# Starting the frequency groups of batches 3 to 7 another 1.2 slots earlier

## The chip, the cores and the metric

One core of a Trainium2 chip runs the whole program. The metric is device time in microseconds (us) of one launch. Names of engines as in the profile: PE is the matmul engine, ACT, DVE and POOL are the scalar, vector and GpSimd engines, SP issues most DMAs.

## The reference

The input x is 8 batches of 3072 rows by 256 columns. Each batch is transformed along its rows to the frequency domain, multiplied there by a complex 256x256 matrix, given a bias, soft-thresholded and transformed back. The 24576 rows that come out pass through a feed-forward block with three maxed branches.

```
X = np.fft.rfft(x, axis=1);  Xr, Xi = X.real, X.imag
Yr = Xr @ w_r - Xi @ w_i + b_r
Yi = Xr @ w_i + Xi @ w_r + b_i
Y* = sign(Y*) * maximum(abs(Y*) - 0.01, 0)
y = np.fft.irfft(Yr + 1j * Yi, n=3072, axis=1)        # 24576 x 256 over all batches
h = maximum(maximum(y @ w1, y @ w2), y @ w3)          # 768 wide
out = h @ w_out
```

## The kernel before

**Tiling.** A batch's main loop has 48 slots (`SLOTS`): 8 chunks of 384 rows, and per chunk 6 blocks of 128 of the 768 hidden columns. In a slot PE does an up product into a tile `pu` (two halves of 6 matmuls, L184 to L186, with a relu by ACT at L1142 between them, which overwrites `pu`) and the down products (`pd`) of an earlier block. The maximum of three branches is taken by two relus and additions folded into the weights. `h` is taken out of `pu` by ACT (L1150) or, every third block, DVE (L1146), and split into two half-precision parts `hh`.

**The transform, between the slots.** A length of 3072 is done as 96 x 32. For batch b, in four steps:

- `stage_a` (L612): the 96-point part for one of 8 pieces of x: 12 matmuls of 48 rows (L625) into two tiles `pa`, emptied by two ACT copies `aq` (L632) and stored to DRAM. Before it DVE and ACT combine and split the piece (`xq` L575, `xhl`).
- `load_a`, `split_a` (`ab`, L694 and L697) and `stage_b` (L792): the 32-point part of a group of frequencies, 16 matmuls into one tile `px`. Four readers empty it: ACT `tt` and `s` (L805), DVE `tt` and `s` (L808). A batch has 12 groups k.
- `stage_w`, `stage_w2`: the weights, three small products into two tiles `py`, read by ACT `cs` (L883) and by DVE `u` (L893), which also adds the bias (L899) and applies the threshold (L837, L839); `finish_w` splits `u` into `vb`, first half on ACT, second on DVE.
- `stage_q` (L960): for every two groups, 12 matmuls into two tiles `pz`, emptied by two ACT copies `zs` (L966) and stored to DRAM. From there the main loop of the next 48 slots takes them in by chunk: `load_z`, `split_z` (`zh` on ACT, `zl` on DVE, then moves `ze<-zl` on SP), `inverse` (`pi` L1091, two tiles per chunk), then `y`, `yh`, `yl`.

**Buffers.** The 8 accumulation banks are three tags: `up` 3 (the tiles `pu`), `dn` 2 (`pd`), and `ff` 3. The tiles `px`, `py`, `pz`, `pa` and `pi` all go through `ff_tile` and so share the three `ff` buffers in the order in which they are issued: a tile gets the buffer of the third `ff` tile before it, when all readers of that one are through.

**What sets the order.** There is no dynamic choice. A table `events` holds (position in slots, function, argument), filled by `at`; `run_until(pos)` issues what is due at thirds of a slot. Second halves of splits wait in `later` for a third or two. Every engine then runs its own list in that order. Two rules of the table matter here (DFT batch b sits in the main loop's slots (b-1)*48 on; its x pieces one batch earlier):

- x pieces of batches 3 to 7, i = 0 to 7: base p = (b-2)*48 + 5.6*i; `stage_a` at p+1.
- groups k of batches 3 to 7: base p = (b-1)*48 - 1.2 + 2.72*(k+2); `stage_b` of group k+1 at p+1, `stage_w` of k at p+2, `stage_w2` at p+2.4, `finish_w` of k-1 at p+1.6, `split_a` of k+1 at p-2.2, `stage_q` of k-1 at p+4 (it acts for every second group), `load_a` of k+3 at p.

`load_z`, `split_z` and `inverse` are called in the main loop itself, at fixed blocks of a chunk, and are in no table.

Of the kernel before, what the change touches and what calls it, by code (L numbers as in the profile page):

```python
# [101 lines left out]
def fourier_maxout_kernel(  # L102
# [13 lines left out]
    SLOTS = NCH * NF  # L116
# [371 lines left out]
    def at(pos, fn, i, k=None, n=None):  # L488
        if n is None or 0 <= k < n:
            events.append((pos, len(events), fn, i))  # L490
# [487 lines left out]
    for q in range(EARLY, NB * NCH):  # L978
        b, i = divmod(q, NCH)
        p = i if b == 1 else 9 + 5.2 * i if b == 2 else (b - 2) * SLOTS + 5.6 * i  # L980
# [5 lines left out]
        if q >= HALF_X:  # L986
            p = 9 + 5 * i if b == 3 else (b - 3) * SLOTS + 5.5 * i + 5
# [3 lines left out]
                at(p + 1, scale_m, b)  # L991
    for b in range(1, NB):
        for k in range(-2, NJP + 1):
            p = 8 + 2.13 * (k + 2) if b == 1 else (b - 1) * SLOTS - (1.2 if b > 2 else 0.4) + 2.72 * (k + 2)
            for d, fn, i in (
                (0, load_a, k + 3), (-2.2 if b > 2 else -1.6, split_a, k + 1), (1.6, finish_w, k - 1),
                (1, stage_b, k + 1), (4 if k < NJP else 3, stage_q, k - 1), (2, stage_w, k), (2.4, stage_w2, k),
            ):
                at(p + d, fn, b * NJP + i, i, NJP)
            if k == -2:  # L1000
                at(p - (2.5 if b > 2 else 0), load_a, b * NJP)
# [530 lines left out]
```

## Time and profile before

| | |
|---|---|
| median of 3 runs | 1742.68 us (1740.84 to 1744.57) |
| profiled execution | 1737.65 us, its span 1735.9 us |
| PE busy | 1713.4 us, 99% of the span, granted clock 1.0 |
| DVE busy | 1269.0 us, 73% |
| ACT busy | 1169.1 us, 67% |
| POOL busy | 292.2 us, 17% |
| main loop's period | 207.18 us a batch (776.12 to 983.30 for the same `pa` block), 4.316 us a slot |

The main loops of batches 2, 3, 4 and 5 (545 to 752, 752 to 959, 959 to 1166 and 1166 to 1372 us) repeat one pattern: in each the groups of the next batch and the x pieces of the batch after that are run. The loop of batch 6 (1372 to 1569 us) has groups but no x pieces, the last one (1569 us on) neither. An engine that is busy 99% of the span shows what bounds the kernel; for the others the idle time before an instruction counts only where PE waits for what that instruction frees or makes.

### The profile page before, as it was taken

The page shows a single profiled execution, that of the slowest core. Times are in us where ns is not written, and L with a number is a line of the kernel's source. Part 1 is how long each engine was busy: PE and PEld are TensorE (multiplying, and loading weights), DVE is VectorE, ACT ScalarE, POOL GpSimd, SP SyncE. Part 2 cuts the span into 40 slices and gives each one's busy share as a digit, 9 for nine tenths or more (in the row PEclk, how much of TensorE's full clock was granted, in tenths as well). Part 3 has the DMA queues.
Part 4 walks back from the last instruction along what each step waited for, and adds up shares of the span by engine and source line. Part 5 has one row for each costly group of instructions (what it writes and reads, how often), then busy time and mean ns, then how long its engine had stood idle before and what let it go on. Part 6 is the DMA issues. An engine that isn't in the chain of part 4 may idle for free.

```text
span 1735.9 us, 42087 instructions
## 1 busy us (share of the span) xinstructions
PE 1713.4 (99%) x16171; PEld 1278.0 (74%) x16171; DVE 1269.0 (73%) x2690; ACT 1169.1 (67%) x2493; POOL 292.2 (17%) x523
## 2 busy tenths in 40 slices
PE   8999999999999999999999999999999999999998
PEld 5866777677776777777777777777777777778998
DVE  2887887687866788678876688757787467667775
ACT  4567676677766777667775777667776566666775
POOL 2101012111221212211221111211222110110000
PEclk9999999999999999999999999999999999999999
DMA  9866565577646767466766567555753443422121
GB/s 294 249 183 195 161 167 162 159 183 190 186 120 178 181 185 192 133 175 177 191 168 167 156 178 204 159 143 153 191 160 106 121 126 104 122 78 64 56 60 34
DMA packets 203863, 269.61 MB, mean 155 GB/s; under 512 B 31438, under 2 KB 153262, under 8 KB 203566
## 3 DMA queue, kind: packets, MB, share of 16 engines
q1 hardware_dynamic: 171294, 193.34, 42.4%
q0 software_dynamic: 24736, 66.62, 12.0%
q10 hardware_dynamic: 7632, 6.95, 1.4%
q8 instruction: 128, 2.10, 0.5%
q14 instruction: 73, 0.60, 0.1%
HBM read 124.31 MB, written 75.50 MB: 115 GB/s over the span
## 4 chain that ended last, share of the span: by engine, by line
PE 81%; DVE 9%; DMA 5%; ACT 4%; issue 1%; SPq 1%; ACTq 0%; POOL 0%; DVEq 0%; POOLq 0%
PE pu L184 11%; PE pu L186 11%; PE pu L185 11%; PE pd L184 8%; PE pd L186 8%; PE pd L185 8%; PE py L184 3%; PE py L186 3%; PE py L185 3%; PE pi L1091 2%; PE px L792 2%; PE pa L625 2%; PE pz L960 2%; PE pu L1176 2%; PE pa L642 1%
## 5 line engine op out<-in xcount | busy, mean ns | idle before, releaser
L184 PE MATMUL pu<-yh,wuh 128*128 128x384 f16 x1344 | 438.6, 326 | 0.0
L186 PE MATMUL pu<-yh,wul 128*128 128x384 f16 x1344 | 438.0, 326 | 0.0
L185 PE MATMUL pu<-yl,wuh 128*128 128x384 f16 x1344 | 438.0, 326 | 0.0
L184 PE MATMUL pd<-woh,hh 128*128 128x256 f16 x1152 | 314.1, 273 | 0.6 <-ACT o L1273 0.4
L186 PE MATMUL pd<-woh,hh 128*128 128x256 f16 x1152 | 313.8, 273 | 0.1
L185 PE MATMUL pd<-wol,hh 128*128 128x256 f16 x1152 | 313.8, 273 | 0.0
L176 DVE TENSOR_TENSOR hh<-h,hh 128x384 f16<-128x384 f32 x336 | 185.9, 553 | 110.2 <-ACT hh L175 109.9
L1142 ACT ACTIVATE pu<-pu 128x384 f32<-128x384 f32 x336 | 160.7, 478 | 145.1 <-PE pu L186 135.1
L175 ACT ACTIVATE hh<-h 128x384 f16<-128x384 f32 x336 | 174.4, 519 | 70.2 <-DVE h L1146 64.9
L186 PEld LDWEIGHTS <-wul 128*128 128x128 f16 x1344 | 131.4, 98 | 86.7
L635 POOL DMA_DIRECT2D a_d<-aq x160 | 94.9, 597 | 584.9 <-ACT aq L632 573.5
L184 PEld LDWEIGHTS <-wuh 128*128 128x128 f16 x1344 | 131.3, 98 | 83.3 <-issue 21.6
L1278 POOL DMA_DIRECT2D out_dram<-o x189 | 104.5, 559 | 449.2 <-ACT o L1273 446.0
L185 PEld LDWEIGHTS <-wuh 128*128 128x128 f16 x1344 | 131.4, 98 | 62.5 <-issue 1.0
L1150 ACT ACTIVATE h<-pu 128x384 f32<-128x384 f32 x226 | 109.4, 484 | 47.1 <-PE pu L186 42.7
L184 PE MATMUL py<-wch,tt 128*128 128x256 f16 x504 | 137.4, 273 | 0.6 <-ACT aq L632 0.3
L186 PE MATMUL py<-wch,tt 128*128 128x256 f16 x504 | 137.3, 273 | 0.0
L185 PE MATMUL py<-wcl,tt 128*128 128x256 f16 x504 | 137.3, 272 | 0.0
L184 PEld LDWEIGHTS <-hh 128*128 128x128 f16 x1152 | 112.6, 98 | 33.0 <-issue 11.8
L185 PEld LDWEIGHTS <-hh 128*128 128x128 f16 x1152 | 112.7, 98 | 21.5 <-issue 0.5
L1105 DVE SCALAR_TENSOR_TENSOR y<-pi,ye 128x192 f32<-128x192 f32 x252 | 110.4, 507 | 21.8 <-ACT ye L1099 21.6
L186 PEld LDWEIGHTS <-hh 128*128 128x128 f16 x1152 | 112.6, 98 | 13.8 <-DVE hh L176 0.4
(288 smaller groups left out, 3551.0 us busy)
## 6 DMA issues: line engine op xcount, KB each, us to landing
zq<-z_d SPq DMA_DIRECT2D x63, 384.0 KB, 4.7
out_dram<-o POOLq DMA_DIRECT2D x189, 128.0 KB, 3.5
ab<-a_d SPq DMA_DIRECT2D x84, 256.0 KB, 4.3
ab<-ab SPq DMA_DIRECT2D x336, 64.0 KB, 2.8
vb<-vb SPq DMA_DIRECT2D x308, 64.0 KB, 2.9
z_d<-zs POOLq DMA_DIRECT2D x70, 256.0 KB, 3.9
xm<-in_x_dram SPq DMA_DIRECT2D x40, 384.0 KB, 4.3
a_d<-aq POOLq DMA_DIRECT2D x160, 96.0 KB, 3.3
```

Of the source, the lines that this page charges most:

```text
L175: nc.scalar.activation(out=hi, in_=src, func=AF.Copy)
L176: later(lambda: nc.vector.tensor_tensor(out=lo, in0=src, in1=h, op=ALU.subtract))
L184: nc.tensor.matmul(o, lh, rh, start=start, stop=False, **kw)
L185: nc.tensor.matmul(o, lh, rl, start=False, stop=False, **kw)
L186: st["mm"] = nc.tensor.matmul(o, ll, rh, start=False, stop=stop, **kw)
L625: st["mm"] = nc.tensor.matmul(pa[r][64 * h:64 * h + 64], ft[rows, t], xt[rows, i, h], start=t == i, stop=t == 1,)
L635: nc.gpsimd.dma_start(out=av[1 - r, :, :, n:n + 512], in_=o[64 * h:64 * h + 48])
L792: nc.tensor.matmul(pv[:, h, :, g // 2, g % 2], ah[:, g // 2, g % 2, h * P:(h + 1) * P], mb_sb[:, i, 4 * kb + g].rearrange("p (c m) -> p c ...
L1105: nc.vector.scalar_tensor_tensor(out=yv[:, e], in0=pv[:, 0], scalar=(1 - 2 * e) * Y_SCALE, in1=ev, op0=ALU.mult, op1=ALU.add,)
L1142: st["act"] = nc.scalar.activation(out=p, in_=p, func=AF.Relu)
L1150: st["act"] = nc.scalar.activation(out=h32, in_=p, func=AF.Relu, scale=H_SCALE)
L1278: nc.gpsimd.dma_start(out=out_v[b, c, t + i], in_=o[:, i])
```

## The change

One number of the table changes, in line 994. All seven steps of a group move by it, for batches 3 to 7 alone; the x pieces, the chunk's own steps and batches 1 and 2 stay where they are.

```
-            p = 8 + 2.13 * (k + 2) if b == 1 else (b - 1) * SLOTS - (1.2 if b > 2 else 0.4) + 2.72 * (k + 2)
+            p = 8 + 2.13 * (k + 2) if b == 1 else (b - 1) * SLOTS - (2.4 if b > 2 else 0.4) + 2.72 * (k + 2)
```

Counted in slots from the start of a 48-slot loop, the x pieces' `stage_a` stand at 1, 6.6, 12.2, 17.8, 23.4, 29.0, 34.6 and 40.2 in both. The five `stage_q` that lie among them stand at 13.68, 19.12, 24.56, 30.0 and 35.44 before, and at 12.48, 17.92, 23.36, 28.8 and 34.24 after. The places where one of these meets a `stage_a` are called meetings 1 to 5 here. At meetings 1 and 2 `stage_a` stays ahead, at 3, 4 and 5 `stage_q` is now first.

The first place is ACT in the loop of batch 3, at meeting 3, from the end of one block's split to the copies out of `pa` and `pz`. Before:

```order
L178 ACTIVATE zh<-zq,s0u 96x1024
L1150 ACTIVATE h_12794<-pu 128x384
L694 ACTIVATE ab<-ab 128x512
L175 ACTIVATE hh<-h_12794 128x384
L632 ACTIVATE aq<-pa 128x512 x2
L178 ACTIVATE vb<-u,s0v 128x512
L1142 ACTIVATE pu<-pu 128x384
L178 ACTIVATE tt<-px 128x2x256
L805 ACTIVATE s<-px 128x256
L175 ACTIVATE hh<-h_12875 128x384
L175 ACTIVATE tt<-s 128x2x128
L966 ACTIVATE zs<-pz,s1v 128x512 x2
```

The two copies out of `pa` come first, and `vb`, `tt`, `s` and the copies out of `pz` follow. After the change, the same engine and meeting:

```order
L175 ACTIVATE hh<-h_12753 128x384
L178 ACTIVATE vb<-u,s0v 128x512
L1142 ACTIVATE pu<-pu 128x384
L178 ACTIVATE zh<-zq,s0u 96x1024
L178 ACTIVATE tt<-px 128x2x256
L805 ACTIVATE s<-px 128x256
L1150 ACTIVATE h_12821<-pu 128x384
L966 ACTIVATE zs<-pz,s1v 128x512
L175 ACTIVATE hh<-h_12821 128x384
L966 ACTIVATE zs<-pz,s1v 128x512
L175 ACTIVATE tt<-s 128x2x128
L632 ACTIVATE aq<-pa 128x512 x2
```

`vb`, the chunk's `zh`, `tt` and `s` now stand ahead of the copies out of `pz`, and those ahead of the copies out of `pa`.

The second place is DVE at the same meeting, from the read of `py` (L893) to the second half of `vb` (`xhl` are the halves of an x piece, `ab` that of a group's input, `zl` that of a chunk, h and `hh` those of a hidden block). Before:

```order
L893 SCALAR_TENSOR_TENSOR u<-py,s1x,cs 128x512
L899 ISA u,mxu<-u,bias_ri 128x512
L899 ISA mxu 128x1
L837 TENSOR_SCALAR t<-u 128x512
L839 ISA u,mxu<-t,u 128x512
L839 ISA mxu 128x1
L179 SCALAR_TENSOR_TENSOR zl<-zq,s0u,zh 96x1024
L697 SCALAR_TENSOR_TENSOR ab<-ab 128x512
L176 TENSOR_TENSOR hh<-h_12794,hh 128x384
L179 SCALAR_TENSOR_TENSOR vb<-u,s0v,vb 128x512
L179 SCALAR_TENSOR_TENSOR tt<-px,tt 128x2x256
```

After the change:

```order
L893 SCALAR_TENSOR_TENSOR u<-py,s1x,cs 128x512
L179 SCALAR_TENSOR_TENSOR xhl<-xq,xx,xhl 112x512
L899 ISA u,mxu<-u,bias_ri 128x512
L899 ISA mxu 128x1
L179 SCALAR_TENSOR_TENSOR xhl<-xq,xx,xhl 112x512
L837 TENSOR_SCALAR t<-u 128x512
L697 SCALAR_TENSOR_TENSOR ab<-ab 128x512
L839 ISA u,mxu<-t,u 128x512
L839 ISA mxu 128x1
L176 TENSOR_TENSOR hh<-h_12753,hh 128x384
L179 SCALAR_TENSOR_TENSOR vb<-u,s0v,vb 128x512
L179 SCALAR_TENSOR_TENSOR zl<-zq,s0u,zh 96x1024
```

The two `xhl` of the x piece and an `ab` now lie between L893 and the end of the threshold (L839), which ACT's `vb` needs, where before they lay elsewhere.

The third place is PE at meeting 4 of the same loop (`wuh`, `wul` are up weights, the number after a name tells the buffer's tile). Before, the last matmuls of `stage_a` and what follows them:

```order
L625 LDWEIGHTS zeros_72
L625 MATMUL pa_13223<-xhl_13128,zeros_72 64x512
L184 LDWEIGHTS wuh_81
L184 MATMUL pu_13243<-yh_13035,wuh_81 128x384
L185 LDWEIGHTS wuh_81
L185 MATMUL pu_13243<-yl_13036,wuh_81 128x384
```

After the change, the last matmuls of `stage_q` and what follows them:

```order
L960 LDWEIGHTS zeros_72
L960 MATMUL pz_13253<-vb_12885,zeros_72 64x512
L960 LDWEIGHTS zeros_72
L960 MATMUL pz_13253<-vb_12885,zeros_72 64x512
L625 LDWEIGHTS zeros_72
L625 MATMUL pa_13273<-xhl_13162,zeros_72 64x512
```

The 12 matmuls into `pa` now follow those into `pz` with nothing between them, where before each of the two blocks had up or down products behind it.

## Rows read from the trace of the kernel before

**Rows 1.** The page: busy time by engine, and the granted clock over 40 slices.

```profile
PE 1713.4 (99%) x16171; PEld 1278.0 (74%) x16171; DVE 1269.0 (73%) x2690; ACT 1169.1 (67%) x2493; POOL 292.2 (17%) x523
...
PEclk9999999999999999999999999999999999999999
```

**Rows 2.** Waits of PE, 545 to 1565 us: total us, times, longest.

```profile
PE pi L1091 <- DMA ze<-zl: 2.8, 5, 1.1
```

**Rows 3.** Chain of waits, loop of batch 3: start us, us, blocks of `pa` and `pz`.

```profile
776.12 0.94 PE pa L625 x12
...
854.75 0.77 PE pa L625 x12
...
859.02 0.77 PE pz L960 x12
```

**Rows 4.** Timeline of PE at meeting 2: start us, us, then the instruction.

```profile
828.36 0.27 PE L185 MATMUL pd<-wol,hh 128*128 128x256 f16 x1
828.47 0.27 PE L186 MATMUL pd<-woh,hh 128*128 128x256 f16 x1
828.67 0.84 PE L625 MATMUL pa<-xhl,zeros 48*64 48x512 f16 x12
...
832.39 0.63 PE L792 MATMUL px<-mb_all,ab 128*128 128x64 f16 x16
832.86 0.33 PE L184 MATMUL pu<-yh,wuh 128*128 128x384 f16 x1
833.02 0.33 PE L185 MATMUL pu<-yl,wuh 128*128 128x384 f16 x1
...
833.92 0.84 PE L960 MATMUL pz<-vb,zeros 64*64 64x512 f16 x12
```

**Rows 5.** Timeline of ACT, the same stretch: in brackets its wait, and for whom.

```profile
829.55 1.08 ACT L632 ACTIVATE aq<-pa 128x512 f32<-128x512 f32 x2 [1.59 <-PE pa L625]
...
831.87 0.72 ACT L178 ACTIVATE vb<-u,s0v 128x512 f16<-128x512 f32 x1 [1.23 <-DVE mxu L839]
...
836.57 1.25 ACT L966 ACTIVATE zs<-pz,s1v 128x512 f32<-128x512 f32 x2
```

**Rows 6.** Groups of ACT, 752 to 959 us: busy us, mean ns | idle before.

```profile
L175 ACT ACTIVATE hh<-h 128x384 f16<-128x384 f32 x48 | 24.9, 519 | 11.0 <-DVE h L1146 10.2
...
L1142 ACT ACTIVATE pu<-pu 128x384 f32<-128x384 f32 x48 | 23.0, 479 | 17.4 <-PE pu L186 15.9 <-PE pa L625 1.3
...
L1150 ACT ACTIVATE h<-pu 128x384 f32<-128x384 f32 x32 | 15.5, 484 | 6.6 <-PE pu L186 6.0 <-DVE t L837 0.5
...
L178 ACT ACTIVATE vb<-u,s0v 128x512 f16<-128x512 f32 x12 | 8.7, 721 | 8.5 <-DVE mxu L839 8.3
...
L178 ACT ACTIVATE zh<-zq,s0u 96x1024 f16<-96x1024 f32 x7 | 7.9, 1135 | 0.0
...
L694 ACT ACTIVATE ab<-ab 128x512 f16<-128x512 f32 x12 | 7.4, 620 | 0.0
...
L178 ACT ACTIVATE tt<-px 128x512 f16<-128x512 f32 x12 | 7.0, 584 | 0.1
...
L805 ACT ACTIVATE s<-px 128x256 f32<-128x256 f32 x11 | 4.2, 378 | 0.0
```

**Rows 7.** Timeline of DVE at meeting 2.

```profile
826.17 0.73 DVE L179 SCALAR_TENSOR_TENSOR xhl<-xq,xx,xhl 112x512 f16<-112x512 f32 x1
...
829.16 0.74 DVE L893 SCALAR_TENSOR_TENSOR u<-py,s1x,cs 128x512 f32<-128x512 f32 x1
...
831.75 0.08 DVE L839 DVE_READ_ACCUMULATOR2_ANT mxu<- 128x1 f32 x1
...
835.80 0.41 DVE L808 SCALAR_TENSOR_TENSOR s<-px,s 128x256 f32<-128x256 f32 x1
```

**Rows 8.** Groups of DVE, 752 to 959 us.

```profile
L556 DVE TENSOR_REDUCE mxx<-xm 96x1 f32<-96x1024 f32 x8 | 9.7, 1208 | 0.0
...
L1112 DVE TENSOR_TENSOR yl<-y,yh 128x384 f16<-128x384 f32 x16 | 8.9, 557 | 3.3 <-ACT yh L1110 3.2
```

## The prediction

> **What bounds the kernel now.** First the busy times: PE is at work for 99% of the span and its clock stands in the top tenth in all 40 slices [rows 1], so any time that PE stands still is time of the kernel. Next the waits of PE over its steady part: 2.8 us in five waits, all of `pi` for the moved halves `ze` [rows 2]; no tile in the `ff` ring stops PE there for long enough to be listed. Then the chain, for where the blocks stand: at meeting 3 `pa` runs at 854.75 and `pz` 4.3 us later [rows 3]. So a slot (4.316 us) separates them, and the three shared `ff` buffers are emptied in between. Last the timelines of the engines that empty them: ACT's copies of `pa` end at 830.63, 2.0 us after that block began; `pz` begins 3.3 us later, and ACT takes until 837.2 to bring the first `zs` home [rows 4, 5].
>
> **What the change does.** It adds no work and takes none away. A slot is 4.316 us, so all group steps of batches 3 to 7 start 1.2 x 4.316 = 5.2 us earlier against the main loop and against the x pieces. That is just the distance at which `pz` follows `pa` now (4.3 at meeting 3). In slots, `stage_q` minus `stage_a` was 1.48, 1.32, 1.16, 1.0 and 0.84 at the five meetings, and becomes 0.28, 0.12, -0.04, -0.2 and -0.36. `stage_b`'s `px` of an even group stands 0.28 slots before each `stage_q`. So five tiles (one `px`, two `pz`, two `pa`) ask for three buffers within some 3 us, five times in each of the four loops that have both, 20 meetings in all. A tile waits until the third one before it is emptied.
>
> **How much PE work lies between**, from PE's order after the change and the spacing in rows 4 (an up matmul 0.16, a down matmul 0.11, 16 `px` 0.47, a block of 12 some 0.77 [rows 3]):
> - Meeting 1 (`pa`, `px`, 6 up, `pz`): 1.85 us from the end of a `pa` tile to the `pz` tile that takes its buffer.
> - Meeting 2 (`px`, 9 down, `pa`, 3 up, `pz`): 0.9 us for the same pair.
> - Meeting 3 (`px`, 6 up, `pz`, 5 down, `pa`): 0.95 us from `pz` to the second `pa` tile.
> - Meeting 4 (`px`, 15 down, `pz`, `pa`): 0.5 us.
> - Meeting 5 (`pz`, some downs, `pa`): 1.4 us.
>
> **How long a tile takes to be emptied.** From both sides: if ACT is free when a `pz` ends, its first copy alone decides, half of 1.25, so 0.63 and some start, 0.7 us [rows 5]. As it stood at meeting 2, the block began at 833.92 and lasted 0.84, and the first copy was done at 836.57 + 0.63 = 837.2: 2.4 us after the end [rows 4, 5]. `px` took 836.21 - 833.02 = 3.2 us, until DVE's `s` had been through [rows 4, 7]. Nothing waited for these then.
>
> **Meeting 3 step by step**, as ACT's and DVE's order after the change is shown. Count from the end of the `py` that L893 reads. DVE first has `mxx` 1.21 and `yl` 0.56 [rows 8]; then the threshold train from L893 to the read-out of L839, 831.83 - 829.16 = 2.67 [rows 7], now with two `xhl` of 0.73 [rows 7] and an `ab` (about its first half's 0.62 [rows 6]) inside it. Sum 6.5, less 0.1 at each of five joints (two copies of one shape take 1.08 where one takes 0.58 [rows 5, 6]): 6.0. Only then may ACT's `vb` start, which already waited 1.23 us for the same read-out before the change [rows 5]. Behind `vb` in ACT's queue stand the relu of `pu`, `zh`, `tt`, `s`, `h` and the first `zs`: 0.72 + 0.48 + 1.14 + 0.58 + 0.38 + 0.48 + 0.63, less six joints, 3.8 us [rows 5, 6]. The buffer is free after 9.8 us. PE in that time has 12 up, 15 down, 6 up, `px`, 6 up, `pz` and 5 down: 1.9 + 1.6 + 1.0 + 0.5 + 1.0 + 0.85 + 0.55 = 7.4. PE stands 2.4 to 2.5 us. Before, the copies of `pa` stood ahead of `vb`, so the wait of `vb` cost nothing; that cover is what goes. Without that lateness of `vb` (DVE ahead by all of its train) the same queue counts 0.55.
>
> **The other four.**
> - Meeting 2: ACT from the up half's end has relu, `zh`, `ab`, `h`, `tt`, `hh`, `s`, `aq` before the buffer is free, 0.48 + 1.14 + 0.62 + 0.48 + 0.58 + 0.52 + 0.38 + 0.54 less 0.7 = 4.0, and with 0.3 for the half's end to be seen 4.3, against 6 up, `px`, 9 down, `pa`, 3 up = 3.8: at least 0.5. By the slow emptying, 2.4 - 0.9 = 1.5. I take 1.2, since DVE's `tt` and `s` must also free `px`.
> - Meeting 4: 0.7 - 0.5 = 0.2 to 2.4 - 0.5 = 1.9. `vb` with its wait heads ACT's queue here too, so 1.6.
> - Meeting 5: 0 to 1.0; I take 0.6. Meeting 1: 0 to 0.6; I take 0, for `aq` is next on ACT there.
>
> **The sum.** A loop: 0 + 1.2 + 2.5 + 1.6 + 0.6 = 5.9 us; four loops 23.6. The low ends make 0 + 0.5 + 0.55 + 0.2 + 0 = 1.25, or 5 in all; the high ends 0.6 + 1.5 + 2.9 (2.5 and another 0.4 for `px` late as well) + 1.9 + 1.0 = 7.9, or 32. Taken off: the second `pa` of a loop, hard behind a `py` today, is stretched to 0.94 from 0.77 [rows 3], four times 0.17 = 0.7, which the shift parts; and blocks that now join (meeting 4) save an entry of 0.20 - 0.11 [rows 4] each, 0.4. Net +22.5 (+4 to +31). Other parts at nothing: in the loop of batch 6 no `pa` is there to meet; `load_a` and the moves of `ab` and `vb` on SP pass the chunk's loads and delay them by under a microsecond, while those loads have two slots to land; POOL is busy 17% [rows 1]. The waits for `ze` keep their size, since `load_z`, `split_z` and `inverse` have not moved, only the data behind them is ready sooner.
>
> The profiled execution took 1737.65 us (its span 1735.9 and 1.75 around it); 1760.2 after. The median of the runs stands 5.0 above the profiled one, so 1765 is forecast.
>
> **A rule against the trace.** The clock of PE is in its top tenth in every slice, through the waits of up to 1.1 us of today [rows 1, 2], so the sum is made at full clock. The Trainium skill (TensorE: Matmul & The Clock Gate, section "A second HAM failure mode: psum-queue depth-cycling") tells of a kernel that cycled through its accumulation banks, where the many short idles between groups made the clock swing between half and full. The trace of before agrees with no such swing, but it has few such idles.
>
> **The rivals.**
> - No change: ACT and DVE, at 67% and 73% [rows 1], get to the copies early enough and each meeting costs 0.2 or less. Then 20 x 0.2 less 1.1, about +3: 1743 to 1746. For it: the mean loads leave room. Against: the train that holds `vb` is on record [rows 5], and copies stand behind it in a fixed order. 8%.
> - Faster: `pi`'s waits for `ze` (2.8 us [rows 2]) fall away because the last groups' `zs` reach DRAM 5.2 us sooner, and the meetings stay hidden; with the 1.1 above 1742.7 - 3.9 = 1739. It decides if the wait for `ze` hangs on the arrival of z, and not on the position of the split and on the queue of SP; the fixed calls speak against it. 4%.
> - A heavier toll: what is late at a meeting is late at the next, too, and each takes the 2.5 of meeting 3: 20 x 2.5 - 1 = 49, so 1792. For it: in 21 us from meeting to meeting nothing on PE is slack. Against: ACT and DVE have a quarter or more of that time free and catch up. 10%.
> - The clock gives way: a slot after each of 20 meetings at 1.2 GHz instead of 2.4 costs another slot, 20 x 4.3 = 86 on top, about 1850. For it speaks no row of before; 2%.
>
> **How the numbers follow.** The forecast with its sizes has 76%; its own range is 1750 to 1774. The range of 8 in 10 leaves out the faster case, part of no change and most of the heavy tail: 1748 to 1777. About 0.2%, 3.5 us, is what a measurement of this kernel can tell from no change. Slower by more: 76 + 10 + 2 = 88%; within 8%; faster 4%.
>
> **What would show it.** In the profile after, PE must have waits of a `pa` or `pz` (L625, L960) for ACT's `zs` and `aq` or DVE's `s`, four times each, a period of some 212 us apart; the longest, 2 to 3 us, at the `pa` of meeting 3, 23.4 slots or 101 us into each loop; ACT's `vb` there must start right after L839's read-out. The period of the loops of batches 2 to 5 grows by some 6 us, that of batch 6 and the last by nothing, the clock stays and `pi` still waits for `ze`. It is wrong if those blocks run without waits, if the longest is elsewhere, or if time goes to operations that last longer.

## The result, and the profile after

The changed kernel takes 1767.82 us (1767.06 to 1768.97) against 1741.88 for the kernel before on the same chip, a ratio of 1.0144 [1.0128, 1.0160]: 25.9 us slower, where the sum gave 22.5 and the range was 1748 to 1777. On a second chip it was 1768.04 against 1741.81, 1.0159 [1.0143, 1.0175]. The profiled execution took 1768.11 us, its span 1766.3. That of before was 1737.65, below all of its timed runs on that chip, so the two profiles differ by 30 us and the medians by 26.

Busy times in the page of after, beside [rows 1]: work has not grown, but PE's share has fallen and its busy time has risen by 10 us.

```profile
PE 1723.5 (98%) x16171; PEld 1282.3 (73%) x16171; DVE 1270.2 (72%) x2690; ACT 1172.9 (66%) x2493; POOL 300.4 (17%) x523
```

Waits of PE in after, 545 to 1600 us (total, times, longest), where [rows 2] had one line of weight:

```profile
PE pa L625 <- ACT zs L966: 9.3, 4, 2.5
PE pa L625 <- DVE s L808: 6.2, 4, 1.6
PE pi L1091 <- DMA ze<-zl: 1.6, 3, 1.0
PE pz L960 <- ACT aq L632: 1.7, 3, 0.8
PE pz L960 <- DVE s L808: 1.6, 5, 0.5
PE pz L960 <- DMA ze<-zh: 0.5, 1, 0.5
```

19.3 us of waits of `pa` and `pz` are new, and those of `pa` come in fours: each once per loop. Meeting 3 of the loop of batch 3, in the timeline of PE:

```profile
866.39 0.84 PE L960 MATMUL pz<-vb,zeros 64*64 64x512 f16 x12
...
867.61 0.27 PE L185 MATMUL pd<-wol,hh 128*128 128x256 f16 x1
870.38 1.39 PE L625 MATMUL pa<-xhl,zeros 48*64 48x512 f16 x12 [2.50 <-ACT zs L966]
...
872.66 0.53 PE L186 MATMUL pu<-yh,wul 128*128 128x384 f16 x1
```

Five matmuls of a down product, then nothing for 2.5 us. The block of `pa` itself then takes 1.39 instead of 0.84, since its second tile waits for another buffer. The same stretch on ACT:

```profile
866.47 0.72 ACT L178 ACTIVATE vb<-u,s0v 128x512 f16<-128x512 f32 x1 [2.55 <-DVE mxu L839]
867.10 0.47 ACT L1142 ACTIVATE pu<-pu 128x384 f32<-128x384 f32 x1
867.50 1.13 ACT L178 ACTIVATE zh<-zq,s0u 96x1024 f16<-96x1024 f32 x1
...
869.65 0.68 ACT L966 ACTIVATE zs<-pz,s1v 128x512 f32<-128x512 f32 x1
```

and on DVE:

```profile
862.19 0.76 DVE L893 SCALAR_TENSOR_TENSOR u<-py,s1x,cs 128x512 f32<-128x512 f32 x1
...
866.34 0.10 DVE L839 DVE_READ_ACCUMULATOR2_ANT mxu<- 128x1 f32 x1
...
870.47 0.41 DVE L808 SCALAR_TENSOR_TENSOR s<-px,s 128x256 f32<-128x256 f32 x1
```

ACT stood idle for 2.55 us before `vb`, until DVE's read-out was through, and `zs` came home at 870.33; PE began 0.05 us later. The second `pa` tile had to wait for DVE's `s`, at 870.88. The last row of PE shows something that no row shown of before has: an up matmul of 0.53 us where it took 0.33 [rows 4]. By stretches around meeting 3 of the four loops, in after (start and end, length, then busy time of PE, its weight loads, DVE, ACT and POOL; the last three numbers are granted clock, DMA share and GB/s):

```profile
656.00:662.00 6.00, 5.79 (x33) 3.14 (x33) 1.60 (x4) 3.49 (x8) 3.79 (x6) 0.72 0.97 265
870.00:877.00 7.00, 6.62 (x40) 3.88 (x40) 2.14 (x5) 3.63 (x8) 3.79 (x6) 0.76 0.93 246
1086.00:1092.00 6.00, 6.00 (x37) 3.62 (x32) 1.15 (x4) 2.46 (x6) 3.24 (x6) 0.72 0.97 259
1297.00:1303.00 6.00, 4.31 (x39) 2.89 (x39) 2.91 (x6) 4.52 (x10) 3.79 (x6) 1.00 0.68 192
```

In three of four loops the clock fell to half, 1.2 GHz, for some 3.4 us: 0.28 of 6 us or 0.24 of 7 is 1.7 us lost each time. The fourth, the loop of batch 5, differs in its wait too, which is 1.74 us where the other three have 2.5:

```profile
1298.69 0.84 PE L625 MATMUL pa<-xhl,zeros 48*64 48x512 f16 x12 [1.74 <-ACT zs L966]
```

### The profile page after: what moved, and what is told of

Its sections match the earlier page's. It is cut to its first block, busy times and chain, and to the rows that moved or that the text cites. A ratio compares the mean times of both kernels' runs of the same rounds, so it can differ in the third digit from the quotient of the medians.

```text
span 1766.3 us, 42062 instructions
## 1 busy us (share of the span) xinstructions
PE 1723.5 (98%) x16171; PEld 1282.3 (73%) x16171; DVE 1270.2 (72%) x2690; ACT 1172.9 (66%) x2493; POOL 300.4 (17%) x523
## 4 chain that ended last, share of the span: by engine, by line
PE 67%; DVE 16%; ACT 8%; DMA 5%; issue 3%; SPq 1%; ACTq 0%; DVEq 0%; POOL 0%; POOLq 0%
PE pu L184 9%; PE pu L186 9%; PE pu L185 9%; PE pd L184 7%; PE pd L186 7%; PE pd L185 7%; PE py L184 2%; PE py L186 2%; PE py L185 2%; PE pi L1091 2%; PE pu L1176 2%; PE pa L625 2%; DVE y L1105 2%; PE px L792 1%; PE pf L1176 1%
## 5 line engine op out<-in xcount | busy, mean ns | idle before, releaser
L184 PEld LDWEIGHTS <-wuh 128*128 128x128 f16 x1344 | 131.6, 98 | 79.7 <-issue 19.3
L184 PEld LDWEIGHTS <-hh 128*128 128x128 f16 x1152 | 112.6, 98 | 33.0 <-issue 12.2
```

Of the source, the lines that this page charges most:

```text
L184: nc.tensor.matmul(o, lh, rh, start=start, stop=False, **kw)
```

## The experiments

The theory: `pa` and `pz` meet `px` and each other in the three shared `ff` buffers, PE waits for their emptying, longest where `vb` is late behind DVE's train; in some loops the clock falls after that wait. The first rival: the lead itself costs, whatever it meets.

**Only batch 7 early.**

```
- (2.4 if b > 2 else 0.4)
+ (2.4 if b > 6 else 1.2 if b > 2 else 0.4)
```

> Only batch 7 starts 2.4 slots ahead; batches 3 to 6 keep 1.2. The groups of batch 7 run in the loop of batch 6, where no x pieces are processed. Theory (meetings): nothing meets, within 2 us of the kernel before, 1740 to 1744. Rival (the lead itself costs the same per batch): a fifth of 26 us, some 5 us, 1747.

Measured 1742.42 against 1739.76, 1.0015 [1.0005, 1.0024]: 2.7 us, inside the theory's 1740 to 1744 though 0.7 over its 2 us, and below the 5 of the rival. PE has no wait of `pa` or `pz` in it, and the one wait that it lists at length is the old one:

```profile
PE pi L1091 <- DMA ze<-zl: 1.9, 3, 1.3
```

Where the 2.7 lie is not settled; the profile's first L625 is 1.5 us later already, and its last, still ahead of the groups of batch 7, 2.9 us, of the 3.6 by which the spans of the two profiles differ. So most of what the profiles differ by lies before anything that was moved.

**The x pieces early as well**, which restores the distances of before:

```
- p = ... (b - 2) * SLOTS + 5.6 * i
+ p = ... (b - 2) * SLOTS - 1.2 + 5.6 * i
```

> Lead 2.4, and the x pieces of batches 3 to 7 (load, sum, split, stage_a) start 1.2 slots earlier as well, so that stage_q follows stage_a by 1.48 to 0.84 slots as in the kernel before. Theory (meetings): the waits of pa and pz go, 1740 to 1748 us. Rival (the lead itself costs): all of the 26 us stay or more, 1765 to 1775, since the x pieces are early now too.

1743.82 against 1739.76, 1.0024 [1.0014, 1.0033]. 22 of 26 us are gone with the lead unchanged. So it is not the lead but what it meets; the other 4 us are not traced. PE's waits are those for `ze` alone (3.3 us in seven).

**Only `stage_q` back**, `px` and the rest still early:

```
- (4 if k < NJP else 3, stage_q, k - 1)
+ ((4 if k < NJP else 3) + 1.2 * (b > 2), stage_q, k - 1)
```

> Lead 2.4, but stage_q 1.2 slots later within its group, so that pz stands where it stood before; px, py, vb and the loads stay early. Theory (pz beside pa is what fills the ring): px alone beside pa leaves three tiles for three buffers; 1740 to 1750 us, with ACT's vb no longer in front of a pz that PE waits for. Rival (px beside pa, whose DVE readers are slow, or DVE's train at pa is the cause): half of the loss or more stays, 1755 to 1768.

1744.5 against 1739.76, 1.0031 [1.0020, 1.0042]. Taking `pz` alone from the meeting gives back 21 us; `px` beside `pa` does little. What stays is a `py` behind `pa`:

```profile
PE py L184 <- ACT aq L632: 3.5, 4, 1.0
```

**Still further ahead, 3.6 slots.**

```
- (2.4 if b > 2 else 0.4)
+ (3.6 if b > 2 else 0.4)
```

> The groups of batches 3 to 7 start 3.6 slots ahead instead of 2.4, all else as after the change. Theory (meetings in the three shared ff buffers): stage_q now stands 0.92 to 1.56 slots, 4.0 to 6.7 us, ahead of stage_a, so the tiles no longer meet; the 19 us of waits of pa and pz go, PE does not stand still for 2.5 us and keeps its clock: 1740 to 1748 us. Rival (the lead itself costs, because groups run ever earlier against the chunk's own steps and against SP's queue): 1.2 slots cost 26 us, so 2.4 slots cost some 50 us against the kernel before, 1790.

1767.8 against 1739.76, 1.0161 [1.0146, 1.0177]. Neither side was right. The waits of `pa` went, as the theory had it, but the tiles of `stage_q` now met `pi` and `py`, which go through the same three buffers:

```profile
PE pz L960 <- DVE y L1105: 4.6, 3, 2.8
PE py L184 <- ACT cs L883: 3.4, 4, 1.3
...
PE pz L960 <- ACT xhl L178: 2.2, 1, 2.2
```

The theory had looked at one neighbour of `pz` only.

**Half way, 1.8 slots, and the other way, 0.6 slots.**

```
- (2.4 if b > 2 else 0.4)
+ (1.8 if b > 2 else 0.4)      # the second kernel: 0.6
```

> Lead 1.8, halfway between 1.2 and 2.4. stage_q then follows stage_a by 0.88, 0.72, 0.56, 0.40 and 0.24 slots, 3.8 to 1.0 us, at the five meetings. Theory (a tile waits only where less PE work lies between than the emptying takes, up to 2.4 us): meetings 1 and 2 cost nothing, 3 to 5 up to 1.4 us each, and no wait is long enough to make the clock fall: 3 to 14 us more than the kernel before, 1743 to 1754. Rival (each slot of lead costs the same): half of 26, 1753, with the waits spread over all meetings alike.

> Lead 0.6, further from the x pieces on the other side (2.08 to 1.44 slots behind stage_a). Theory (the kernel before has no waits left there but those of pi for ze): no gain from more distance, 1738 to 1745; where py or pi now fall beside pz a few us more. Rival (each slot of lead costs the same): half of 26 us faster than the kernel before, 1727.

1743.97 and 1745.34 against 1741.81: 1.0011 [1.0002, 1.0021] and 1.0021 [1.0011, 1.0030]. From 1.2 to 1.8 the price is 2 us, from 1.8 to 2.4 it is 24. A price per slot of lead is out; the theory's lower end holds at 1.8, and 0.6 lies 0.3 us above what it gave. At 1.8 the wait is `pz` for `aq`, at 0.6 it is a `py` for DVE's `s`:

```profile
PE pz L960 <- ACT aq L632: 2.2, 5, 0.9
```

```profile
PE py L184 <- DVE s L808: 2.4, 4, 0.7
```

**DVE's train parted**: the halves of the x piece are split one slot earlier.

```
- at(p - 1, sum_x, q);  at(p - 0.4 * (q >= HALF_X), split_x, q)
+ at(p - (2 if b > 3 else 1), sum_x, q);  at(p - (1.4 if b > 3 else 0.4 * (q >= HALF_X)), split_x, q)
```

> Lead 2.4, and sum_x and split_x of the x pieces of batches 4 to 7 one slot earlier (stage_a stays): DVE's two xhl then lie ahead of L893 and no longer between it and the read-out of L839, and ab falls behind it; by DVE's rows (0.67 + 0.67 + 0.6) vb starts 1.9 us sooner at meeting 3. Theory (the lateness of vb behind DVE's train makes the largest wait): the wait for zs falls from 2.5 to some 0.5 to 1, the clock stays, meetings 2, 4 and 5 stay: 4 x 1.7 + 5 = 12 us less, 1754 to 1759. Rival (ACT's own queue behind vb, zh and tt, sets the wait): 1.0 us or less a loop is won, 1763 to 1768.

1761.97 against 1740.60, 1.0120 [1.0103, 1.0137]. By the ratios that is some 5 us better than the changed kernel, which was not run on this chip; it lies between what the theory and the rival gave. At meeting 3 of the loop of batch 3 `vb` began 1.9 us ahead of `pz`, where it had begun 0.1 behind it, and the wait went the way that the theory says, from 2.5 to 1.0 us:

```profile
PE pa L625 <- DVE s L808: 4.5, 4, 1.2
PE pa L625 <- ACT zs L966: 3.8, 4, 1.0
PE pz L960 <- ACT aq L632: 2.7, 4, 0.8
```

but the waits of `pz` for `aq` grew from 1.7 to 2.7, and the clock fell four times instead of three, now behind meeting 4 (at 685, 1109 and 1320 us) and once in the loop of batch 1. The lateness of `vb` is shown as the cause of 1.5 of the 2.5 us of the longest wait; the 12 us that the theory wanted were too many, since it took the clock's falls to go with that wait.

**Four `ff` buffers**, with the bank taken from `up`, for both leads.

```
- bufs=2 if tag == "dn" else 3                     # ff 3, up 3, dn 2
+ bufs={"ff": 4, "up": 2, "dn": 2}[tag]            # and bufs=2 for pu
```

> Lead 2.4 with four ff buffers instead of three, the bank taken from up (two instead of three). To be compared with e8, which has the same buffers and lead 1.2. Theory (the ring of three is too short for the tiles that meet): the difference of the two leads falls from 26 us to 8 or less, since the first wait of each meeting has one more buffer; what two up buffers cost is in both. Rival (the tiles meet, but PE waits for operands or for engines that are behind anyway): the difference stays 20 us or more.

> The kernel before (lead 1.2) with four ff buffers and two up buffers: the base for e7. Up tiles then wait for their relu and their reader at every block, so 10 to 100 us more than the kernel before; no theory of the meetings gives its size. Theory: no waits of pa or pz for aq, zs or s.

With lead 1.2 1757.76, 1.0099 [1.0084, 1.0114] against the kernel before, with 2.4 1776.48, 1.0210 [1.0194, 1.0227]: 18.7 us between them. That lies between the two, nearer the rival. The waits of the early one:

```profile
PE pa L625 <- ACT zs L966: 9.4, 4, 2.5
PE pa L625 <- DVE s L808: 4.3, 4, 1.1
...
PE pz L960 <- ACT aq L632: 2.5, 4, 0.6
```

The wait for `zs` is as long as with three. With four buffers the first `pa` of meeting 3 gets one that is long free, but the second gets that of the first `pz`: the wait moves from one tile of the pair to the other. One buffer more was too few here; five were not tried. `pz` and `pa` wait for nothing of the kind at lead 1.2. Part of the 18.7 is not the ring: in the profile of the early kernel the clock falls in all four loops (granted 0.72 from 655 to 661, 870 to 876, 1085 to 1091 and 1300 to 1306 us), in that of the other in none (1.00 from 545 to 1600 us). At 1.7 us a fall that is 6.8 us, so by these two profiles the fourth buffer took the rest from some 21 us (26 less three falls) to some 12.

**The wait filled with work**: matmuls with zero weights into an open `pd` tile between `pz` and `pa` at meeting 3.

```
+ if b > 3 and q4 == 4:
+     for _ in range(20):                              # the second kernel: 14
+         matmul(st["pd"][0][:, 0:D], zeros[:, 0:P], woh[:, 0], start=False, stop=False)
```

> The changed kernel with 20 more matmuls (zero weights, 256 columns, added to an open pd tile, so the sums stay) between pz and pa at meeting 3 of the four loops: 20 x 0.109 = 2.2 us of PE work inside the wait of 2.5 us. Theory (the wait at meeting 3 makes PE's clock fall to half for 3.4 us in three of the four loops, 1.7 us each): the wait is filled, the clock stays at 1.0 after it, and the kernel gets some 5 us faster although it does more work: 1762 to 1764 us against 1768. Rival (the clock falls for another reason, or its fall lies beside waits anyway): no gain, 1768 to 1771, with 0.5 still seen in the granted clock.

> The changed kernel with 14 added matmuls (1.5 us) in the wait at meeting 3, where 20 (2.2 us) were put in before. Theory (a wait of PE of 2.5 us makes the clock fall, and the fall costs 1.7 us each time): the wait is filled by 1.5 us, some 1 us remains, the clock stays at 1.0 behind it; 3 to 6 us faster than the changed kernel on the same chip. Rival (the clock's fall costs nothing of its own): same time within 1 us.

> The changed kernel as it is, for the same chip as the next one: 1764 to 1770 us.

With 20: 1766.25 against 1740.60, 1.0152 [1.0136, 1.0168]; with 14: 1768.33, the changed kernel on the same chip 1768.04, against 1741.81, 1.0151 [1.0134, 1.0168] and 1.0159 [1.0143, 1.0175]. As whole times, no gain: with 20 the time lies between the two sides, and the changed kernel was not run on that chip; with 14 the theory's 3 to 6 us are missed. By loops they say more. With 20 the longest wait at meeting 3 is 0.9 us and the clock stays at 1.0 in all four loops, as in these three:

```profile
660.00:668.00 8.00, 7.00 (x60) 4.90 (x59) 4.27 (x8) 5.38 (x12) 3.78 (x6) 1.00 0.88 246
874.00:881.00 7.00, 6.11 (x52) 4.24 (x52) 3.27 (x7) 4.53 (x10) 3.78 (x6) 1.00 0.91 247
1087.00:1094.00 7.00, 5.99 (x51) 4.16 (x51) 3.27 (x7) 4.55 (x10) 3.78 (x6) 1.00 0.99 264
```

Three loops (from the first `pa` of one to the first of the fourth) then take 640.3 us, 3.8 less than the 644.1 of the changed kernel, though there is 6.5 us more work in them. That execution had lost 5.4 us ahead of these loops, 1.7 of it in a fall of the clock at 109 us; the rest of that stays open, and its whole time, the longest of four (the others took 1765.5 to 1766.8), hides the gain. With 14 a wait of 1.5 us is left and the clock falls in two loops of four. The clearest price comes from the changed kernel run again. Its first loop, the same instructions, once with a fall and once without, by the first `pa` of each loop in the chain of after,

```profile
549.21 0.77 PE pa L625 x12
764.28 0.77 PE pa L625 x12
978.68 0.77 PE pa L625 x12
1193.34 0.77 PE pa L625 x12
```

and in the one run again:

```profile
550.18 0.77 PE pa L625 x12
763.56 0.77 PE pa L625 x12
977.88 0.77 PE pa L625 x12
1192.53 0.77 PE pa L625 x12
```

215.07 us against 213.38, and the clock there 0.72 against

```profile
656.00:662.00 6.00, 4.87 (x39) 3.12 (x39) 2.82 (x6) 4.38 (x10) 3.78 (x6) 1.00 0.92 253
```

The second and third loops, with a fall in both, are 214.40 and 214.32, 214.66 and 214.65. So a fall costs 1.7 us of time, and the same program falls three times in one execution and twice in another. No kernel tried was faster than the one before.

## Why the prediction was right, and where it was not

- **Direction and place held, and so did the size of the loops.** In before, the first `pa` of each loop stands at

```profile
547.11 1.05 PE pa L625 x12
753.99 1.06 PE pa L625 x12
961.16 1.06 PE pa L625 x12
1167.43 1.05 PE pa L625 x12
```

Against these rows the loops of batches 2 to 4 grew by 8.2, 7.2 and 8.4 us, with a fall of the clock in each; without the falls that is 6.2 a loop. The loop of batch 5, by its last `pa`, grew by 4.7. That makes 23.4 us, where 22.5 were summed.
- **That 1767.8 lies 3 us from 1765 is in part luck.** From profile to profile the forecast was 1760.2, and 1768.11 came: 7.9 too little. Three falls of the clock are 5.1 of that, 2.1 were lost ahead of the four loops (549.21 against 547.11), and 0.9 is what the loops took beyond the sum. Against it stands the 5.0 added because the median of before lies above its profile: the median of after lies 0.3 below its own. Nor does the forecast's own low end of 1750 follow from its +4, which gives 1747.
- **Meeting 3 came out step by step.** `py` ended at 860.45, `vb` began at 866.47, 6.0 us later as summed (6.0), and the first `zs` was home 3.9 us after that (3.8). PE stood 2.5 us (2.4 to 2.5), and 0.55 inside the block on top, which the sum left out. In the loop of batch 5 the wait was 1.7. Parting the train showed that `vb`'s lateness makes most of the wait.
- **Meetings 1, 2 and 5** were summed at 0, 1.2 and 0.6. At meeting 2 of this loop PE waited 0.46 for `aq` and 0.29 for `s`, 1.3 with the short stops in the block; at 5 the block took 1.37 for 0.84, so 0.5; at 1 nothing, though in the loop of batch 2 it cost 0.9 (a block of 1.73, 0.49 of it a wait for `s`).
- **Meeting 4 had the right size by the wrong buffer.** 1.6 was priced as `pa` behind `zs`; it was 1.53 behind DVE's `s`, the last reader of `px`, so the agreement is luck. At meeting 3 the first `pa` began with `zs`, before the readers of `px` were through: it took `pz`'s buffer and the second `px`'s, not the other way round. By PE's order, then, a tile did not get the buffer of the third `ff` tile before it there, as the section on the kernel has it.
- **The clock was the mis-sized term.** The sum was made at full clock, and the clock's giving way had 2% at 86 us. It did give way, but behind meeting 3 alone, in two or three loops of four, for 1.7 us each: 3.4 to 5.1 us. The Trainium skill (TensorE: Matmul & The Clock Gate, section "A second HAM failure mode: psum-queue depth-cycling") tells of a kernel that cycles through its accumulation banks and whose short idles between matmul groups make the clock swing between half and full. The trace agrees in kind, with the 0.72 above, and says that here it is a fifth of the loss or less.
- **The waits for `ze`** were said to keep their size; over the same stretch they went from 2.8 [rows 2] to 1.6 us. The loop of batch 6 and the last one took no longer in the profile: the last L625 is 30.6 us later than before, the span 30.4.
- A wait of 1.0 us of `pa` for ACT's `hh` in the loop of batch 1 was in no step.
- **The rivals.** No change, faster and the heavy toll are out by the time. That each slot of lead costs is out by 1.8 slots (2 us) and by the x pieces moved along (4 us).

## What to carry to other kernels

When a table of positions is shifted, list which tiles share a ring of buffers and see how much PE work lies between each pair in the new order; a distance that is shorter than the emptying is a wait, and it recurs with the loop. Look at every user of the ring: a shift that clears one neighbour can run into the next, as 3.6 slots did. To shift one step with its neighbours (the x pieces here) costs little; to shift it through them costs all.

## What was not expected of the hardware

In the changed kernel the clock did not fall during the wait but 1.0, 1.9 and 2.1 us after its end, when PE was at work again: in the loop of batch 3 the down matmuls at 871.70 still took 0.28 us, the up matmul at 872.66 took 0.53. In the loop of batch 2 the wait ended at 656.21, and in the microsecond from 657 the granted clock was 0.61:

```profile
657.00:658.00 1.00, 1.00 (x10) 0.29 (x5) 0.60 (x2) 1.00 (x4) 0.73 (x2) 0.61 1.02 219
```

With 3.6 slots it fell as the wait ended:

```profile
653.60 1.49 PE L960 MATMUL pz<-vb,zeros 64*64 64x512 f16 x10 [2.20 <-ACT xhl L178]
653.00:654.00 1.00, 0.40 (x4) 0.18 (x8) 1.00 (x3) 1.00 (x3) 0.00 (x0) 0.79 0.42 99
```

The length of the wait alone did not tell whether it fell. After 2.5 us at meeting 3 it fell in all three loops that had such a wait in one execution and in two of the three in another. After 1.1 to 1.2 us at meeting 4 of the kernel with the split parted it fell in three loops of four, after the 1.5 us at meeting 4 of the changed kernel in none. With the wait at meeting 3 filled down to 0.9 us it fell behind none. In the profiles of the seven kernels in which PE waits 1.4 us at most in these loops (before, only batch 7 early, the x pieces moved along, `stage_q` back, 1.8 and 0.6 slots, and four buffers at lead 1.2) it stayed at 1.00.
